# v loaded in k's layout, E turned by VectorE in 32x32 blocks, and the product with v in 18 steps of four 32x32 tiles

## The chip, the cores and the metric

The kernel runs on one core of a Trainium2 chip. The metric is the device time of one execution in microseconds, as the median of several runs. TensorE (PE) multiplies matrices, VectorE (DVE) and ScalarE (ACT) work elementwise, GpSimd (POOL) does a few conversions, and SyncE (SP) issues nearly all transfers, which run on 16 shared DMA engines.

## The reference

Two attentions and two feed-forward blocks, one behind the other. The change lies in the first attention, where 32 "pack" queries p attend to 576 tokens.

```python
# q, k, v: (8, 8, 576, 64) = batch, heads, tokens, head size; p: (8, 8, 32, 64)
def sm_attn(qq, kk, vv):
    s = scale * qq @ kk^T
    a = exp(s - max(s));  a = a / (sum(a) + 1e-9)
    return a @ vv
p_packed = sm_attn(p, k, v)              # 32 x 64 per head
out      = sm_attn(q, p_packed, p_packed)
x = out as (4608, 512)
x = (h * cos(h)) @ w_out          with h = x @ w_in          # 512 -> 2048 -> 512
x = (P(h) / (Q(h) + 1e-6)) @ w_out with h = x @ w_in         # 512 -> 2048 -> 512
```

## The kernel before, in words

The first stage takes the 64 (batch, head) pairs in NG = 16 groups of four heads. In a group the four heads lie side by side on the partitions, 32 each, and each step of a matrix product is made of four small matmuls, one for a head, which are placed on different tiles of TensorE's array.

For a group n the steps are these. `load_k` brings k with 18 consecutive tokens a partition: partition 32h + j holds tokens 18j to 18j + 17 of head h, as one run of 4608 bytes. `load_v` brings v in another layout, with tokens on 96 partitions: three transfers of 32 partitions each, in runs of 6 tokens (1536 bytes). `prep` turns k in 32x32 blocks on VectorE (kT). `s1` computes the scores in two halves of 288 tokens (tile `s` in the profile), takes their maximum (mx), scales it (nb), lets ScalarE form E = exp(...) with its sum (sm), and inverts the sum (rd). `et` turns E on TensorE, in six transposes of 128x96 into PSUM, which ScalarE copies to eT. `pv` multiplies eT with v into one PSUM tile of 128x64; ScalarE scales it by rd into pd and pp. `ppt` turns pd on TensorE (pt), and ScalarE puts it into wl, which the next stage reads.

The loop runs these steps shifted against each other: in its round n come the scores of group n + 1, the loads and the turning of k for later groups, `et(n)`, `pv(n - 1)` and `ppt(n - 2)`. Between them stand the steps of the second attention of batch 0 (qT, ppT, sT, aT, al) and, in every second round, the conversion of a weight tile (st, cvf, w1i). Each engine works off its own row of instructions in order; a scheduler makes these rows when the program is built. SyncE's transfers are issued in order too. Buffers are few: three each for kx and vx, two each for kT, E and eT, and two PSUM tiles for scores.

The stage behind it starts with the matmuls `w<-w1i,wl` (L284), which need all of the first stage's PSUM, so all of its groups. The two feed-forward blocks follow and fill the rest of the time.

Of the kernel before, what the change touches and what calls it, by code (L numbers as in the profile page):

```python
# [9 lines left out]
F32 = mybir.dt.float32  # L10
F32R = mybir.dt.float32r
U32 = mybir.dt.uint32
AF = mybir.ActivationFunctionType
# [7 lines left out]
def pack_attention_moe_moe_kernel(  # L21
# [14 lines left out]
    nc = tc.nc  # L36
# [75 lines left out]
    if True:  # L112
# [18 lines left out]

        def load_v(n):
            b, g = divmod(n, G)
            t = wv.tile([96, 4, 6 * D], F32, tag="vx", bufs=3, name="vx")
            for a in range(3):
                nc.sync.dma_start(
                    out=t[32 * a:32 * a + 32],
                    in_=v[b, 4 * g:4 * g + 4].rearrange("h (j a r) d -> a j h (r d)", a=3, r=6)[a],
                )
            vx_t[n] = t  # L140

        def load_kv(n):
# [31 lines left out]
        kT_t = {}  # L174

        def prep(n):
            b, g = divmod(n, G)
            kT = wk.tile([128, NDB, 6, 3, 32], F32, tag="kT", bufs=2, name="kT")
            kx = kx_t.pop(n)
            for e in range(NDB):  # L180
                nc.vector.transpose(
                    out=kT[:, e].rearrange("p r a j -> p a r j"),
                    in_=kx[:, :, 32 * e:32 * e + 32].rearrange("p (a r) i -> p a r i", a=3),
                )
            kT_t[n] = kT.rearrange("p e r a j -> p e (r a j)")

        def scores(ps, lhs, rhs):
            for hf in range(2):
# [22 lines left out]
        E_t, rd_t = {}, {}  # L211

        def s1(n):
            ps = ps0.tile([128, 2, 512], F32, tag="s1", bufs=2, name="s1")
            scores(ps, pT[:, n], kT_t.pop(n))
            mx = wk.tile([128, 1], F32, tag="mx", bufs=2, name="mx")
            nc.vector.tensor_reduce(out=mx, in_=ps[:, :, 0:HS], op=ALU.max, axis=AX.XY)
            nb = wk.tile([128, 1], F32, tag="nb", bufs=2, name="nb")
            nc.vector.tensor_scalar(out=nb, in0=mx, scalar1=-scale, scalar2=None, op0=ALU.mult)
            E = wk.tile([128, 6, 96], F32, tag="E", bufs=2, name="E")  # L220
            sm = wk.tile([128, 1], F32, tag="sm", bufs=2, name="sm")
            nc.scalar.activation(
                out=E.rearrange("p (t r) x -> p t (r x)", t=2),
                in_=ps[:, :, 0:HS], func=AF.Exp, scale=scale, bias=nb, accum_out=sm,
            )
            rd = wk.tile([128, 1], F32, tag="rd", bufs=3, name="rd")
            nc.vector.tensor_scalar(out=sm, in0=sm, scalar1=1e-9, scalar2=None, op0=ALU.add)
            nc.vector.reciprocal(out=rd, in_=sm)
            E_t[n], rd_t[n] = E, rd

        et_t = {}

        def et(n):
            E = E_t.pop(n)
            ps = ps0.tile([96, 2, 512], F32, tag="et", name="et")
            for r in range(6):
                o = 128 * (r % 3)
                nc.tensor.transpose(ps[:, r // 3, o:o + 128], E[:, r, :], ident)
            eT = wv.tile([96, 6, 128], F32, tag="eT", bufs=2, name="eT")
            nc.scalar.activation(out=eT.rearrange("p (t r) m -> p t (r m)", t=2), in_=ps[:, :, 0:384], func=AF.Copy)  # L240
            et_t[n] = eT

        pd_t = {}
# [1 line left out]
        def pv(n):  # L245
            eT, vx = et_t.pop(n), vx_t.pop(n)
            ps = ps0.tile([128, D], F32, tag="pv", name="pv")

            for r in range(6):
                for h in range(4):  # L250
                    pace[0] = nc.tensor.matmul(
                        out=ps[32 * h:32 * h + 32],
                        lhsT=eT[:, r, 32 * h:32 * h + 32],
                        rhs=vx[:, h, r * D:r * D + D],
                        start=(r == 0),
                        stop=(r == 5),
                        tile_position=(0, 32 * h),
                    )
            rd = rd_t.pop(n)
            pd = wk.tile([128, 2, D], F32, tag="pd", bufs=2, name="pd")  # L260
            nc.scalar.activation(
                out=pd, in_=ps.unsqueeze(1).to_broadcast([128, 2, D]), func=AF.Copy, scale=rd
            )
            pd_t[n] = pd
            nc.scalar.activation(out=pp[:, n], in_=ps, func=AF.Copy, scale=rd)
# [192 lines left out]
        for i in range(at_ld0):  # L458
# [1 line left out]

        tg0 = {"qT": ("kT", 2), "aT": ("E", 2)}
        at = attn2_steps(
            0, wk, lambda nm: ps0.tile([128, 2, 512], F32, tag="s1", bufs=2, name=nm), tg0, lambda: None
        )
        s1(0)
        prep(1)
        for n in range(NG + 2):
            if n >= 3:
                next(at, 1)
            if n + 1 < NG:  # L470
                s1(n + 1)
            if n + 3 < NG:
                load_k(n + 3)
            if n + 2 < NG:
                load_v(n + 2)
                prep(n + 2)
            if n < NG:
                et(n)
            if 1 <= n <= NG:
                pv(n - 1)  # L480
            if n >= 2:
                ppt(n - 2)
            if n % 2 and n <= 2 * EARLY:
                conv_next()
# [429 lines left out]
```

## Time and profile before

| what | us |
|---|---|
| median of 3 runs (lowest, highest) | 1663.2 (1661.97, 1664.64) |
| the profiled execution: time | 1665.62 |
| its span, first to last instruction | 1663.6 |
| TensorE busy | 1595.3 (96%) |
| VectorE busy | 1252.1 (75%) |
| ScalarE busy | 1200.8 (72%) |
| first stage: first scores, first matmul of the next stage | 7.34, 110.26 |

The span is what the trace covers; the time of the same execution is 2.0 us longer. A busy share is an average over stages with different limits, so the first stage has to be read by itself. An instruction's time reaches from its start to its end on its engine; neighbours on one engine overlap a little, so the distance from one start to the next says more on a row of them.

### The profile page before, as it was taken

The page shows a single profiled execution, that of the slowest core. Times are in us where ns is not written, and L with a number is a line of the kernel's source. Part 1 is how long each engine was busy: PE and PEld are TensorE (multiplying, and loading weights), DVE is VectorE, ACT ScalarE, POOL GpSimd, SP SyncE. Part 2 cuts the span into 40 slices and gives each one's busy share as a digit, 9 for nine tenths or more (in the row PEclk, how much of TensorE's full clock was granted, in tenths as well). Part 3 has the DMA queues.
Part 4 walks back from the last instruction along what each step waited for, and adds up shares of the span by engine and source line. Part 5 has one row for each costly group of instructions (what it writes and reads, how often), then busy time and mean ns, then how long its engine had stood idle before and what let it go on. Part 6 is the DMA issues. An engine that isn't in the chain of part 4 may idle for free.

```text
span 1663.6 us, 25747 instructions
## 1 busy us (share of the span) xinstructions
PE 1595.3 (96%) x9792; PEld 1353.8 (81%) x9792; DVE 1252.1 (75%) x1934; ACT 1200.8 (72%) x1973; POOL 158.2 (10%) x120
## 2 busy tenths in 40 slices
PE   6789988999999999999999999999999999999997
PEld 3446668999999999999998888888888888888886
DVE  5745568777868777868558888888888888888886
ACT  3467657676768677768668877877777778787875
POOL 1014330112111112121000000000000000000000
PEclk9889999999999999999999999999999999999999
DMA  9957774344444444445292101010110202020010
GB/s 273 246 151 241 245 213 134 116 142 133 137 133 125 139 144 133 136 127 179 63 303 110 54 24 51 26 51 26 37 40 3 74 1 76 1 76 1 12 40 26
DMA packets 98427, 176.40 MB, mean 106 GB/s; under 512 B 11648, under 2 KB 42880, under 8 KB 98304
## 3 DMA queue, kind: packets, MB, share of 16 engines
q1 hardware_dynamic: 97984, 174.23, 34.4%
q8 instruction: 77, 1.26, 0.3%
q10 hardware_dynamic: 320, 0.52, 0.1%
q14 instruction: 46, 0.38, 0.1%
HBM read 114.36 MB, written 60.36 MB: 105 GB/s over the span
## 4 chain that ended last, share of the span: by engine, by line
PE 75%; DVE 8%; ACT 5%; issue 2%; DMA 2%; POOL 0%; SPq 0%; DVEq 0%; ACTq 0%; POOLq 0%
PE h L773 24%; PE o L860 24%; PE y L634 16%; PE h L580 8%; PE w L307 1%; PE s L192 1%; DVE r L606 1%; ACT r L610 1%; DVE g L612 1%; DVE gl L67 1%; ACT r L611 1%; PE w L284 1%; DVE wq L67 1%; DVE qT L343 1%; DVE sT L383 1%
## 5 line engine op out<-in xcount | busy, mean ns | idle before, releaser
L634 PE MATMUL y<-gh,w1o 128*128 128x288 f32 x2048 | 440.7, 301 | 4.1 <-ACT gh L66 2.6
L773 PE MATMUL h<-x,w 128*128 128x512 f32 x1728 | 422.2, 393 | 0.0
L773 PEld LDWEIGHTS h<-x,w 128*128 128x128 f32 x1728 | 324.2, 188 | 74.3
L634 PEld LDWEIGHTS y<-gh,w1o 128*128 128x128 f32 x2048 | 338.5, 190 | 17.0 <-issue 7.7
L860 PE MATMUL o<-w,g2h 128*128 128x512 f32 x1152 | 332.9, 393 | 1.2 <-ACT g2h L791 1.2
L634 PE MATMUL y<-gl,w1o 128*128 128x288 f32 x1024 | 300.6, 300 | 8.3 <-DVE gl L67 8.2
L860 PEld LDWEIGHTS o<-w,g2h 128*128 128x128 f32 x1152 | 216.2, 188 | 51.1 <-ACT g2h L791 2.1
L580 PE MATMUL h<-ah,wq 128*128 128x288 f32 x1024 | 231.8, 302 | 14.0 <-DVE g L612 13.2
L634 PEld LDWEIGHTS y<-gl,w1o 128*128 128x128 f32 x1024 | 194.6, 190 | 15.5 <-DVE gl L67 11.8
L860 PE MATMUL o<-w,g2l 128*128 128x512 f32 x576 | 199.9, 393 | 0.0
L806 ACT ACTIVATE sq<-h 128x512 f32<-128x512 f32 x144 | 87.6, 608 | 154.6 <-PE h L773 154.6
L580 PEld LDWEIGHTS h<-ah,wq 128*128 128x128 f32 x1024 | 173.1, 190 | 24.2 <-issue 19.2
L808 DVE SCALAR_TENSOR_TENSOR ab<-sq,coef,ab 128x512 f32<-128x512 f32 x144 | 108.2, 751 | 66.0 <-ACT ab L807 65.8
L612 DVE SCALAR_TENSOR_TENSOR g<-h,r 128x576 f32<-128x576 f32 x128 | 95.6, 753 | 79.6 <-ACT r L611 79.0
L580 PE MATMUL h<-al,wq 128*128 128x288 f32 x512 | 151.7, 296 | 0.0
L605 ACT ACTIVATE u<-h,coef 128x576 f32<-128x576 f32 x128 | 94.3, 739 | 74.0 <-PE h L580 73.5
L817 DVE SCALAR_TENSOR_TENSOR ab<-ab,y 128x512 f32<-128x512 f32 x144 | 99.5, 691 | 48.7 <-ACT y L814 48.7
L860 PEld LDWEIGHTS o<-w,g2l 128*128 128x128 f32 x576 | 108.2, 188 | 24.6
L606 DVE SCALAR_TENSOR_TENSOR r<-u,h 128x576 f32<-128x576 f32 x128 | 95.3, 748 | 38.6 <-ACT u L605 38.2
L67 DVE TENSOR_TENSOR gl<-g,gh 128x576 fp32r<-128x576 f32 x128 | 99.7, 780 | 30.4 <-ACT gh L66 28.5
L809 ACT ACTIVATE c<-h,coef 128x512 f32<-128x512 f32 x144 | 114.3, 794 | 8.5 <-DVE g2l L797 8.4
L66 ACT ACTIVATE gh<-g 128x576 fp32r<-128x576 f32 x128 | 87.3, 682 | 40.9 <-DVE g L612 38.2
(98 smaller groups left out, 2315.6 us busy)
## 6 DMA issues: line engine op xcount, KB each, us to landing
x<-yd SPq DMA_DIRECT2D x36, 512.0 KB
w<-w2d SPq DMA_DIRECT2D x68, 256.0 KB
st<-in_moe_w_in_dram SPq DMA_DIRECT2D x32, 512.0 KB
st<-in_moe_w_out_dram SPq DMA_DIRECT2D x32, 512.0 KB
wq<-wd SPq DMA_DIRECT2D x56, 256.0 KB
wd<-wev SPq DMA_DIRECT2D x48, 256.0 KB
kx<-in_k_dram SPq DMA_DIRECT2D x16, 576.0 KB
vx<-in_v_dram SPq DMA_DIRECT2D x48, 192.0 KB
```

Source lines behind the costliest of these rows:

```text
L67: lo_eng.tensor_tensor(out=lo, in0=src, in1=hi.bitcast(F32), op=ALU.subtract)
L580: last_h[0] = nc.tensor.matmul(out=ps[:, u, 0:HS], lhsT=wq[:, g, a, o:o + 128], rhs=a_t[b, g][c][:, hf * HS:hf * HS + HS], start=(i == 0), ...
L605: nc.scalar.activation(out=u, in_=ph, func=AF.Identity, bias=coef[:, 6:7])
L606: nc.vector.scalar_tensor_tensor(out=r, in0=u, scalar=RND, in1=ph, op0=ALU.subtract, op1=ALU.subtract)
L612: nc.vector.scalar_tensor_tensor(out=gt, in0=ph, scalar=2.0 * math.pi, in1=r, op0=ALU.mult, op1=ALU.mult)
L634: nc.tensor.matmul(out=y_t[d][:, 0:HS], lhsT=w1o_s[f // 4][a][:, f % 4, 128 * d:128 * d + 128], rhs=gs[c][:, u], start=(first and u == 0 a ...
L773: nc.tensor.matmul(out=ps, lhsT=w2_s[f][:, 0, a, 128 * kk:128 * kk + 128], rhs=x_t[t, c, kk], start=(i == 0), stop=(i == 3 * NKD - 1),)
L806: nc.scalar.activation(out=sq, in_=ph, func=AF.Square)
L808: nc.vector.scalar_tensor_tensor(out=ab, in0=sq, scalar=coef[:, 5:6], in1=ab, op0=ALU.mult, op1=ALU.add)
L809: nc.scalar.activation(out=c1, in_=ph, func=AF.Identity, scale=coef[:, 3:4], bias=coef[:, 2:3])
L817: nc.vector.scalar_tensor_tensor(out=ab, in0=ab, scalar=QC, in1=y0, op0=ALU.add, op1=ALU.mult)
L860: nc.tensor.matmul(out=o_t[s], lhsT=g2_t[n][a][:, 128 * s:128 * s + 128], rhs=w2_s[f][:, 1, c], start=(f == 0 and i == 0), stop=(f == NFC ...
```

## The change

v is loaded like k: one transfer of 128 partitions with runs of 4608 bytes. E keeps the token order of k, as 18 blocks of 32 columns, and VectorE turns it in 32x32 blocks, from SBUF to SBUF, which leaves the tokens of each head on that head's 32 partitions, as v now has them. The six transposes on TensorE, their PSUM tile and the copy by ScalarE go. The product with v is then a sum over 18 steps with 32 tokens of each head, in place of 6 steps with 96: 72 matmuls with a contraction of 32 rows in place of 24 with 96, each head on its own rows and columns of the array. k is turned by one instruction instead of two, without the reordering of tokens. There is a third PSUM tile for scores, and `et(n)` stands ahead of `prep(n + 2)` in the loop.

```diff
--- before.py
+++ after.py
@@ -131,12 +131,8 @@
 
         def load_v(n):
             b, g = divmod(n, G)
-            t = wv.tile([96, 4, 6 * D], F32, tag="vx", bufs=3, name="vx")
-            for a in range(3):
-                nc.sync.dma_start(
-                    out=t[32 * a:32 * a + 32],
-                    in_=v[b, 4 * g:4 * g + 4].rearrange("h (j a r) d -> a j h (r d)", a=3, r=6)[a],
-                )
+            t = wv.tile([128, C, D], F32, tag="vx", bufs=3, name="vx")
+            nc.sync.dma_start(out=t, in_=v[b, 4 * g:4 * g + 4].rearrange("h (j c) d -> (h j) c d", c=C))
             vx_t[n] = t
 
         def load_kv(n):
@@ -174,15 +170,11 @@
         kT_t = {}
 
         def prep(n):
-            b, g = divmod(n, G)
-            kT = wk.tile([128, NDB, 6, 3, 32], F32, tag="kT", bufs=2, name="kT")
-            kx = kx_t.pop(n)
-            for e in range(NDB):
-                nc.vector.transpose(
-                    out=kT[:, e].rearrange("p r a j -> p a r j"),
-                    in_=kx[:, :, 32 * e:32 * e + 32].rearrange("p (a r) i -> p a r i", a=3),
-                )
-            kT_t[n] = kT.rearrange("p e r a j -> p e (r a j)")
+            kT = wk.tile([128, NDB, C, 32], F32, tag="kT", bufs=2, name="kT")
+            nc.vector.transpose(
+                out=kT.rearrange("p e c j -> p c e j"), in_=kx_t.pop(n).rearrange("p c (e i) -> p c e i", e=NDB)
+            )
+            kT_t[n] = kT.rearrange("p e c j -> p e (c j)")
 
         def scores(ps, lhs, rhs):
             for hf in range(2):
@@ -211,16 +203,16 @@
         E_t, rd_t = {}, {}
 
         def s1(n):
-            ps = ps0.tile([128, 2, 512], F32, tag="s1", bufs=2, name="s1")
+            ps = ps0.tile([128, 2, 512], F32, tag="s1", bufs=3, name="s1")
             scores(ps, pT[:, n], kT_t.pop(n))
             mx = wk.tile([128, 1], F32, tag="mx", bufs=2, name="mx")
             nc.vector.tensor_reduce(out=mx, in_=ps[:, :, 0:HS], op=ALU.max, axis=AX.XY)
             nb = wk.tile([128, 1], F32, tag="nb", bufs=2, name="nb")
             nc.vector.tensor_scalar(out=nb, in0=mx, scalar1=-scale, scalar2=None, op0=ALU.mult)
-            E = wk.tile([128, 6, 96], F32, tag="E", bufs=2, name="E")
+            E = wk.tile([128, C, 32], F32, tag="E", bufs=2, name="E")
             sm = wk.tile([128, 1], F32, tag="sm", bufs=2, name="sm")
             nc.scalar.activation(
-                out=E.rearrange("p (t r) x -> p t (r x)", t=2),
+                out=E.rearrange("p (t c) j -> p t (c j)", t=2),
                 in_=ps[:, :, 0:HS], func=AF.Exp, scale=scale, bias=nb, accum_out=sm,
             )
             rd = wk.tile([128, 1], F32, tag="rd", bufs=3, name="rd")
@@ -231,13 +223,8 @@
         et_t = {}
 
         def et(n):
-            E = E_t.pop(n)
-            ps = ps0.tile([96, 2, 512], F32, tag="et", name="et")
-            for r in range(6):
-                o = 128 * (r % 3)
-                nc.tensor.transpose(ps[:, r // 3, o:o + 128], E[:, r, :], ident)
-            eT = wv.tile([96, 6, 128], F32, tag="eT", bufs=2, name="eT")
-            nc.scalar.activation(out=eT.rearrange("p (t r) m -> p t (r m)", t=2), in_=ps[:, :, 0:384], func=AF.Copy)
+            eT = wv.tile([128, C, M], F32, tag="eT", bufs=2, name="eT")
+            nc.vector.transpose(out=eT, in_=E_t.pop(n))
             et_t[n] = eT
 
         pd_t = {}
@@ -246,15 +233,16 @@
             eT, vx = et_t.pop(n), vx_t.pop(n)
             ps = ps0.tile([128, D], F32, tag="pv", name="pv")
 
-            for r in range(6):
+            for c in range(C):
                 for h in range(4):
+                    r = slice(32 * h, 32 * h + 32)
                     pace[0] = nc.tensor.matmul(
-                        out=ps[32 * h:32 * h + 32],
-                        lhsT=eT[:, r, 32 * h:32 * h + 32],
-                        rhs=vx[:, h, r * D:r * D + D],
-                        start=(r == 0),
-                        stop=(r == 5),
-                        tile_position=(0, 32 * h),
+                        out=ps[r],
+                        lhsT=eT[r, c],
+                        rhs=vx[r, c],
+                        start=(c == 0),
+                        stop=(c == C - 1),
+                        tile_position=(32 * h, 32 * h),
                     )
             rd = rd_t.pop(n)
             pd = wk.tile([128, 2, D], F32, tag="pd", bufs=2, name="pd")
@@ -460,7 +448,7 @@
 
         tg0 = {"qT": ("kT", 2), "aT": ("E", 2)}
         at = attn2_steps(
-            0, wk, lambda nm: ps0.tile([128, 2, 512], F32, tag="s1", bufs=2, name=nm), tg0, lambda: None
+            0, wk, lambda nm: ps0.tile([128, 2, 512], F32, tag="s1", bufs=3, name=nm), tg0, lambda: None
         )
         s1(0)
         prep(1)
@@ -471,11 +459,11 @@
                 s1(n + 1)
             if n + 3 < NG:
                 load_k(n + 3)
+            if n < NG:
+                et(n)
             if n + 2 < NG:
                 load_v(n + 2)
                 prep(n + 2)
-            if n < NG:
-                et(n)
             if 1 <= n <= NG:
                 pv(n - 1)
             if n >= 2:
```

TensorE's row around groups 4 to 6 of the first stage. `s_` tiles are scores (from kT in the first attention, from qT in the second), et the transposes of E, pv the product, pt the turning of pd. Before:

```order
L202 MATMUL s_375<-kT,pT 32x288 x16
L238 MATMUL et<-ident,E 96x128 x6
L251 MATMUL pv<-vx,eT 32x64 x24
L271 MATMUL pt<-ident,pd 128x128
L202 MATMUL s_467<-kT,pT 32x288 x16
L238 MATMUL et<-ident,E 96x128 x6
L251 MATMUL pv<-vx,eT 32x64 x24
L271 MATMUL pt<-ident,pd 128x128
L202 MATMUL s_544<-qT,ppT 32x288 x16
L202 MATMUL s_565<-kT,pT 32x288 x16
```

The same place now:

```order
L194 MATMUL s_435<-kT,pT 32x288 x16
L239 MATMUL pv<-vx,eT 32x64 x72
L259 MATMUL pt<-ident,pd 128x128
L194 MATMUL s_565<-kT,pT 32x288 x16
L239 MATMUL pv<-vx,eT 32x64 x72
L259 MATMUL pt<-ident,pd 128x128
L194 MATMUL s_680<-qT,ppT 32x288 x16
L194 MATMUL s_701<-kT,pT 32x288 x16
```

The six transposes between the scores and the product are gone, and the product has three times as many matmuls; nothing else moved.

VectorE's row around groups 4 and 5. mx and nb are the maximum and its scaling, sm and rd the sum of E (which waits for ScalarE's exp) and its inverse, cvf the weight conversion, qT a step of the second attention. Before:

```order
L217 TENSOR_REDUCE mx<-s_375 128x1
L343 STREAM_TRANSPOSE qT<-qx 128x18x2x32
L219 TENSOR_SCALAR nb<-mx 128x1
L79 TENSOR_SCALAR cvf<-st_136 128x512
L84 SCALAR_TENSOR_TENSOR cvf<-st_136,cvf 128x512
L227 TENSOR_SCALAR sm<-sm 128x1
L228 RECIPROCAL rd<-sm 128x1
L217 TENSOR_REDUCE mx<-s_467 128x1
L181 STREAM_TRANSPOSE kT<-kx 128x3x6x32 x2
L219 TENSOR_SCALAR nb<-mx 128x1
L227 TENSOR_SCALAR sm<-sm 128x1
L228 RECIPROCAL rd<-sm 128x1
```

The same place now:

```order
L209 TENSOR_REDUCE mx<-s_435 128x1
L331 STREAM_TRANSPOSE qT<-qx 128x18x2x32
L211 TENSOR_SCALAR nb<-mx 128x1
L219 TENSOR_SCALAR sm<-sm 128x1
L220 RECIPROCAL rd<-sm 128x1
L79 TENSOR_SCALAR cvf<-st_131 128x512
L84 SCALAR_TENSOR_TENSOR cvf<-st_131,cvf 128x512
L227 STREAM_TRANSPOSE eT<-E 128x576
L209 TENSOR_REDUCE mx<-s_565 128x1
L174 STREAM_TRANSPOSE kT<-kx 128x18x2x32
L211 TENSOR_SCALAR nb<-mx 128x1
L219 TENSOR_SCALAR sm<-sm 128x1
```

A turn of E stands at the end of each group's round, and the weight conversion, which stood between nb and sm, now stands behind rd. The kT that is turned between mx and nb belongs to the next group in the rounds of groups 5 and 7, and to the one behind the next from group 8 on, in both kernels. Behind the first stage the rows of all engines are the same in both.

## Rows read from the trace of the kernel before

**Rows 1.** Stretches in us: busy time (instructions) of each engine, granted clock, DMA share, GB/s.

```profile
15.00:20.00 5.00, 4.97 (x54) 2.25 (x50) 2.78 (x8) 2.60 (x4) 0.00 (x0) 0.70 1.02 406
...
41.80:45.30 3.50, 3.50 (x35) 1.50 (x31) 0.00 (x0) 0.65 (x4) 0.00 (x0) 0.51 1.06 267
...
20.00:95.00 75.00, 59.05 (x1089) 32.60 (x1079) 50.26 (x104) 33.99 (x88) 7.71 (x6) 0.89 0.98 246
...
85.00:90.00 5.00, 5.00 (x38) 2.17 (x38) 0.96 (x2) 0.52 (x3) 0.00 (x0) 0.54 1.00 202
...
110.00:1663.60 1553.60, 1513.98 (x8336) 1309.46 (x8336) 1187.77 (x1793) 1154.04 (x1850) 145.39 (x105) 0.99 0.31 96
```

**Rows 2.** Timeline of SyncE's transfers: first issue us, us to the last, count.

```profile
10.89 0.33 SPq L129 DMA_DIRECT2D kx<-in_k_dram  x1
...
81.10 15.05 SPq L136 DMA_DIRECT2D vx<-in_v_dram  x12
```

**Rows 3.** Waits of SyncE, 8 to 96 us: us in total, times, longest.

```profile
SPq L136 <- DMA vx<-in_v_dram: 11.0, 18, 1.2
```

**Rows 4.** Timeline of TensorE: start us, us, tile, count [idle before <-releaser].

```profile
7.34 3.99 PE L202 MATMUL s<-kT,pT 32*32 32x288 f32 x32 [7.34 <-DVE pT L169]
...
95.03 2.14 PE L202 MATMUL s<-kT,pT 32*32 32x288 f32 x32
97.10 0.86 PE L238 MATMUL et<-ident,E 128*96 128x128 f32 x6
97.89 0.88 PE L251 MATMUL pv<-vx,eT 96*32 96x64 f32 x48
98.70 0.33 PE L271 MATMUL pt<-ident,pd 128*128 128x128 f32 x1
98.96 2.14 PE L202 MATMUL s<-kT,pT 32*32 32x288 f32 x32
...
110.26 2.79 PE L284 MATMUL w<-w1i,wl 128*64 128x512 f32 x5 [0.58 <-ACT wl L275]
```

**Rows 5.** Timeline of VectorE, columns as in rows 4.

```profile
13.10 1.44 DVE L181 STREAM_TRANSPOSE kT<-kx 128x576 f32<-128x576 f32 x2 [4.25 <-DMA kx<-in_k_dram]
14.46 0.72 DVE L217 TENSOR_REDUCE mx<-s 128x1 f32<-128x576 f32 x1
...
20.90 1.44 DVE L181 STREAM_TRANSPOSE kT<-kx 128x576 f32<-128x576 f32 x2 [1.48 <-DMA kx<-in_k_dram]
...
93.98 1.43 DVE L181 STREAM_TRANSPOSE kT<-kx 128x576 f32<-128x576 f32 x2
95.33 0.11 DVE L219 TENSOR_SCALAR nb<-mx 128x1 f32<-128x1 f32 x1
96.40 0.15 DVE L227 TENSOR_SCALAR sm<-sm 128x1 f32<-128x1 f32 x1 [0.96 <-ACT E L222]
96.59 0.16 DVE L228 RECIPROCAL rd<-sm 128x1 f32<-128x1 f32 x1
...
101.17 0.76 DVE L217 TENSOR_REDUCE mx<-s 128x1 f32<-128x576 f32 x1 [0.79 <-PE s L202]
```

**Rows 6.** Waits of VectorE from its first to its last maximum, 14.4 to 101.3 us.

```profile
DVE kT L181 <- DMA kx<-in_k_dram: 7.4, 4, 3.8
DVE sT L366 <- PE s L202: 7.0, 2, 5.0
DVE mx L217 <- PE s L202: 6.9, 5, 4.5
DVE sm L227 <- ACT E L222: 6.0, 7, 1.0
DVE qT L343 <- DMA qx<-in_q_dram: 1.9, 1, 1.9
```

**Rows 7.** Groups by line, 0 to 110 us: busy us, mean ns | idle before.

```profile
L251 PEld LDWEIGHTS pv<-vx,eT 96*32 96x32 f32 x768 | 12.9, 117 | 12.4 <-issue 7.4 <-ACT E L222 3.0 <-ACT pp L265 1.5
```

## The prediction

> **What bounds the kernel now.** I read the stretches first. From 110 us to the end TensorE is busy 1514.0 of 1553.6 us [rows 1]: that is the two feed-forward stages, where the diff touches nothing, and the order of all five engines behind the first stage is the same row for row in both kernels. So whatever the change does it does before 110.26 us, when the first matmul of the next stage starts [rows 4], and it moves the end by as much as it moves that start.
>
> Inside the first stage the next view is the DMA's share. From 20 to 95 us it is 0.98 at 246 GB/s [rows 1]: the transfers bound most of the stage, at a poor rate. The rate depends on what moves. The k load issued at 10.89 us is not there until 20.90 [rows 2, 5]; ahead of it in the queue stand another k load and two weight loads, so 15 to 20 us is k and weights, and it runs at 406 GB/s. From 81.10 on SyncE issues twelve v pieces and nothing else [rows 2]; 85 to 90 us runs at 202 GB/s with the same full share [rows 1]. v, in pieces of 32 partitions and 1.5 KB runs, goes at half the rate of k in 128 partitions and 4.5 KB runs. SyncE itself waits on earlier landings, 18 times on v alone [rows 3], and VectorE and TensorE stand behind it. VectorE's waits from its first maximum to its last are 7.4 us for k, 1.9 us for q, and 7.0 + 6.9 us for scores that TensorE gave late [rows 6]. Only the last groups, from some 93 us, run at TensorE's pace: scores 2.07 us (95.03 to 97.10), transposes of E 0.79, the product with v 0.81, pt 0.26, together 3.93 us a group [rows 4].
>
> **The change, part by part.**
> *Loads.* v is 16 x 576 KB = 9.44 MB: 46.7 us at 202 GB/s, 23.2 us at k's 406. The transfers lose about 23 us of work, and with it most of their hold: the 18.5 MB moved from 20 to 95 us would take 45 us at 406. The bounds are 202 (no change) and 406; I take 406, since v then has k's own layout. The k load of group 1 lands sooner too: VectorE turns it at 13.10 us after a wait of 4.25 [rows 5], with v(0) and parts of v(1) ahead of it or beside it; px has landed by 7 us (the first scores, behind its transposition, start at 7.34 [rows 4]), and from there two loads of 576 KB at 406 GB/s are 2.9 us. So kT(1) starts at about 10.0 and the first maximum at 11.4 in place of 14.46; the first scores end at 11.33 [rows 4], just in time.
>
> *TensorE.* 0.79 us of transposes go. The product has 72 matmuls in place of 24. The rows count each f32 matmul twice: 48 records start within 0.81 us (97.89 to 98.70), 67 ns for each of a tile's 12 [rows 4]. A tile now has 36: 2.43 us. The low bound is the streaming alone: scores pass 8 records of 288 columns per tile in 2.07 us, so 64 columns are 57 ns and 36 records 2.07 us. I take 2.43, the nearer row. TensorE's round is then 2.07 + 2.43 + 0.26 = 4.76 us, 0.83 more than now.
>
> *ScalarE.* Sixteen evacuations go; ScalarE is not what anyone is behind for long, so I count nothing.
>
> *VectorE.* It gets sixteen turns of E. Two turns of 128x576 take 1.35 us from start to next start (93.98 to 95.33 [rows 5]), so 0.68 each. kT is one instruction instead of two over the same elements: nothing. The order shows two more things: the weight conversion now stands behind rd instead of between nb and sm, so VectorE waits for ScalarE's exp in ten of the first fifteen groups (groups 2 to 7 and 11 to 14) instead of seven. One such wait is 0.96 us [rows 5]; ten are 9.6 us against 6.0 now [rows 6].
>
> *The sum.* VectorE's time from first to last maximum is 101.17 - 14.46 = 86.7 us. Off go 7.4 + 1.9 + 7.0 + 6.9 = 23.2 us of waits for transfers and late scores; on come 15 x 0.68 = 10.2 us of turns and 3.6 us of exp waits: 77.3 us. The last maximum starts at 11.4 + 77.3 = 88.7 us. Behind it stands the tail, now 9.2 us (last scores done at 101.1, next stage at 110.26 [rows 4]). With its waits kept it becomes 9.2 - 2 x 0.79 + 3 x (2.43 - 0.81) = 12.5 us; bare work, three products and what follows the last one now, is about 10. I take 11. That gives 99.7 us if nothing else stalls.
>
> Two things will. VectorE's round without extra work is 0.76 + 1.35 + 1.07 + 0.19 + 0.16 + 0.68 = 4.2 us [rows 5], below TensorE's 4.76: in some six plain groups VectorE waits up to 0.55 us, 3.3 us at most and nothing where kT runs two groups ahead; I take 2. And after a gap TensorE's granted clock falls: 0.51 in 41.8 to 45.3 us [rows 1], the lower of its two levels, 1.2 of 2.4 GHz, right behind a wait for v. A spell of 3.5 us costs up to 1.7 us; I put one on the path. The stage then ends at about 103.4 us, **7 us sooner**.
>
> The profiled execution took 1665.62 us for a span of 1663.6; the median of the runs is 1663.2, 2.4 below it. Taking 7 us off the median gives 1656.2 us. About 0.2%, 3.3 us, can be told from no change.
>
> **A rule against it.** Now four tiles of the product share rows and differ in columns; then they differ in both, and all four add into one PSUM bank. The scores already do just that, four 32x32 tiles into the bank of a half, and 32 records pass in 2.07 us; one after another they would need four times that, 8.3 us [rows 4]. So I price the tiles as side by side. The Trainium skill's "TensorEngine Tiling (Array Packing)", Restrictions and Gotchas, says that different row tiles cannot access the same PSUM bank at the same time; by it the product would be serial, which is the last rival below. This case's scores disagree with it, at 2.07 us against 8.3.
>
> **Rivals.**
> *VectorE and TensorE hold each other up.* Both now have some 80 us of work before the last maximum (TensorE: 11.4 + 17 x 2.07 + 12 x 0.26 + 13 x 2.43 = 81.3 us on the clock, against 88.7). Five stalls or low-clock spells of 1.7 us instead of one bring the stage to its present end: 1660 to 1666. For it: the exp wait stands bare in VectorE's in-order row, and around groups 4 to 7 kT is turned only one group ahead. Against: TensorE's gaps of today are waits for transfers.
>
> *The work packs better.* With no low-clock spell, the product at 2.07 us, a tail of 10, the stage ends at 97 to 99.5, the first matmuls of the next stage no longer run at the low clock: 11 to 14 us off, 1649 to 1652.
>
> *v stays slow.* If v's 202 GB/s is not from its layout, the transfers end where they end now, and the tail grows by 1 to 3 us: 1663 to 1666. Against it: k's rate in the same queue.
>
> *The product is dearer than the room.* TensorE's whole row is 11.4 + 35.2 + 3.1 + 0.5 + 2.1 us and sixteen products: 52.3 + 16 x p. At p = 3.6 us the stage ends where it ends now; above that the kernel is slower. A load of weights for the product lasts 117 ns [rows 7]; if a tile's 36 loads are not hidden behind its own matmuls, p = 36 x (0.117 + 0.067) = 6.6 us, the stage ends at 158, and the time is about 1711. Fully serial tiles would be 144 x 67 ns = 9.7 us, end 207.5: 1760. For it: a load then serves a third of the rows, so there are three times as many. Against: the 48 records of today pass at 17 ns each, load and matmul together, and the scores' 32x32 tiles run four abreast.
>
> **How the numbers follow.** My forecast, 3.4 to 11 us off: 0.56. Better packing: 0.14. Mutual holding: 0.16. v slow: 0.05. The product too dear: 0.09, of which serial tiles 0.03. Faster by over 0.2%: 0.56 + 0.14 = 0.70. Slower: 0.09 and part of v slow, 0.11. Within: 0.19. The range reaches from the better packing's end, 1648, to 1664, where mutual holding and slow v are mostly in; beyond it lie the dear product and some of those two, under 0.2.
>
> **What would show it.** Right: k and v loads alike, windows of 5 us near 400 GB/s in the first 20 us and a DMA share well below 0.9 after 30; VectorE's waits for k and q gone and those for exp near ten; VectorE busy 80% or more from 11 to 90 us; the product's 144 records in 2.1 to 2.5 us; the next stage's first matmul at 100 to 107 us. Wrong: a product over 3 us, or v windows still near 200 GB/s, or TensorE's clock at half in more than three spells before 100 us.

## The result and the profile after

The changed kernel takes 1674.87 us (median; 1674.34 to 1680.97), the kernel before 1662.59 (1659.55 to 1664.64): a ratio of 1.0078, 95% interval 1.0050 to 1.0106. It is **slower by 12 us** where 7 us faster was predicted. The profiled execution took 1674.34 us for a span of 1672.5.

The stretches of the changed kernel, with the columns of [rows 1]:

```profile
15.00:20.00 5.00, 5.00 (x72) 2.41 (x68) 3.52 (x8) 2.93 (x5) 0.00 (x0) 0.71 1.03 417
14.50:18.00 3.50, 3.50 (x36) 1.55 (x32) 2.60 (x5) 2.11 (x3) 0.00 (x0) 0.52 1.04 421
20.00:95.00 75.00, 59.49 (x2025) 41.14 (x2017) 53.57 (x100) 23.33 (x74) 6.41 (x5) 0.93 0.68 234
24.70:28.10 3.40, 3.40 (x45) 1.95 (x37) 2.76 (x5) 0.57 (x2) 1.28 (x1) 0.50 0.53 144
41.80:45.20 3.40, 3.40 (x114) 3.07 (x109) 2.08 (x3) 0.14 (x1) 0.00 (x0) 0.50 0.50 197
86.10:89.50 3.40, 3.08 (x37) 1.57 (x41) 1.09 (x3) 1.40 (x6) 0.00 (x0) 0.51 0.34 102
113.40:116.90 3.50, 3.25 (x114) 2.78 (x102) 0.00 (x0) 0.55 (x3) 0.00 (x0) 0.51 0.02 5
122.00:1672.50 1550.50, 1511.07 (x8337) 1306.42 (x8336) 1187.84 (x1793) 1151.58 (x1851) 144.99 (x105) 0.99 0.31 97
```

The transfers did what was predicted: 417 GB/s with v among them, and a DMA share of 0.68 from 20 to 95 us where it was 0.98 [rows 1]. Behind the first stage the order is that of before, and TensorE is busy 1511.1 of 1550.5 us there. But the product breaks off, again and again. TensorE's timeline, columns as in [rows 4]; it shows the start, the last quarter and the end of the stage:

```profile
19.84 1.96 PE L239 MATMUL pv<-vx,eT 32*32 32x64 f32 x127
24.41 0.52 PE L239 MATMUL pv<-vx,eT 32*32 32x64 f32 x17 [2.62 <-issue]
...
100.32 1.72 PE L239 MATMUL pv<-vx,eT 32*32 32x64 f32 x91
103.88 0.86 PE L239 MATMUL pv<-vx,eT 32*32 32x64 f32 x44 [1.84 <-issue]
...
106.89 2.19 PE L239 MATMUL pv<-vx,eT 32*32 32x64 f32 x144
109.01 0.33 PE L259 MATMUL pt<-ident,pd 128*128 128x128 f32 x1
109.83 0.64 PE L239 MATMUL pv<-vx,eT 32*32 32x64 f32 x31 [0.49 <-ACT pp L253]
113.19 3.05 PE L239 MATMUL pv<-vx,eT 32*32 32x64 f32 x113 [2.72 <-issue]
...
122.60 2.67 PE L272 MATMUL w<-w1i,wl 128*64 128x512 f32 x8 [0.58 <-ACT wl L263]
```

Where nothing breaks it and the clock is full, the product passes in 2.12 us (106.89 to 109.01). Elsewhere it breaks off in its middle, with its operands there since its first record, and TensorE stands for 0.6 to 2.7 us on "issue", a wait for nothing that another engine does. The next stage starts at 122.60 in place of 110.26 [rows 4]: 12.3 us later, as much as the medians differ. The two profiled spans differ by less, 8.9 us: what stands behind that start took 1549.9 us in this execution and 1553.3 in that of before, a difference within the spread of either kernel's runs. The waits of the stage, for TensorE (0 to 123 us) and VectorE (11 to 115 us), columns as in [rows 6]:

```profile
PE pv L239 <- issue: 14.8, 8, 2.7
...
PE pv L239 <- ACT pp L253: 5.3, 5, 2.1
...
PE s L194 <- issue: 2.6, 2, 2.0
```

```profile
DVE sm L219 <- ACT E L214: 11.5, 14, 1.0
DVE mx L209 <- PE s L194: 11.2, 6, 4.7
DVE kT L174 <- DMA kx<-in_k_dram: 3.4, 4, 1.9
DVE sT L354 <- PE s L194: 2.6, 2, 1.5
```

VectorE's waits for q went and those for k fell from 7.4 us [rows 6] to 3.4; those for exp grew, as predicted, though in 14 places where ten were counted. Its waits for scores did not go (13.8 us, 13.9 before [rows 6]): TensorE is late again, from a new cause. On issue it waits 17.4 us in ten places. In the trace of before there is one such wait up to 111 us:

```profile
PE pv L251 <- issue: 1.7, 1, 1.7
```

**Where the breaks lie.** Stretches of the changed kernel from 0 to just before a break; the counts in brackets behind the first two busy times are TensorE's matmul and load records:

```profile
0.00:24.40 24.40, 11.47 (x223) 5.75 (x223) 11.84 (x27) 4.32 (x8) 2.55 (x7) 0.93 0.90 320
0.00:35.40 35.40, 20.32 (x476) 11.76 (x477) 20.04 (x40) 6.79 (x17) 3.83 (x8) 0.90 0.87 307
0.00:40.60 40.60, 23.53 (x604) 13.96 (x604) 22.14 (x45) 8.78 (x23) 5.11 (x9) 0.92 0.88 311
...
0.00:103.80 103.80, 75.64 (x2383) 50.16 (x2384) 68.17 (x131) 29.36 (x87) 10.26 (x13) 0.93 0.70 241
0.00:113.10 113.10, 81.74 (x2636) 54.67 (x2637) 74.06 (x141) 32.63 (x98) 12.89 (x15) 0.94 0.69 236
```

From break to break there are 253, 128, ..., 253 matmul records, with as many loads: all ten breaks lie whole multiples of 127 matmuls apart, within 1, that is of some 254 records, whether a product or a score is cut. That is a property of the instruction stream, not of data. The queues of the page say what comes in such pieces (packets, MB, share), of before and then of after:

```profile
q8 instruction: 77, 1.26, 0.3%
```

```profile
q8 instruction: 88, 1.44, 0.4%
```

Eleven packets more, 0.18 MB or some 16 KB each, for 1440 matmuls and as many loads more (9792 and 11232 of each on the two pages): a packet for 262 records. Hence **theory A**: TensorE's instructions come in blocks of some 256, and the change makes it use them up faster than they come. **Theory B**, the prediction's own rival: the engines hold each other up (exp waits that stand bare, one pv buffer, low clock), and the number of records costs only its passing.

### The profile page after: what moved, and what is told of

Same layout as the page of the kernel before. It is cut to its first block, busy times and chain, and to the rows that moved or that the text cites. A ratio compares the mean times of both kernels' runs of the same rounds, so it can differ in the third digit from the quotient of the medians.

```text
span 1672.5 us, 28544 instructions
## 1 busy us (share of the span) xinstructions
PE 1599.3 (96%) x11232; PEld 1366.5 (82%) x11232; DVE 1261.9 (75%) x1934; ACT 1186.0 (71%) x1957; POOL 157.9 (9%) x120
## 4 chain that ended last, share of the span: by engine, by line
PE 77%; DVE 10%; ACT 6%; issue 3%; DMA 2%; POOL 1%; SPq 1%; DVEq 0%; ACTq 0%; POOLq 0%
PE h L761 24%; PE o L848 23%; PE y L622 15%; PE h L568 8%; PE pv L239 2%; PE s L194 2%; PE w L295 1%; PE s L184 1%; ACT r L598 1%; DMA yd<-yh 1%; DVE r L594 1%; DVE gl L67 1%; ACT r L599 1%; DVE g L600 1%; PE w L272 1%
## 5 line engine op out<-in xcount | busy, mean ns | idle before, releaser
L568 PE MATMUL h<-ah,wq 128*128 128x288 f32 x1024 | 230.6, 301 | 14.1 <-DVE g L600 13.4
```

The costliest lines, as they stand in the source:

```text
L568: last_h[0] = nc.tensor.matmul(out=ps[:, u, 0:HS], lhsT=wq[:, g, a, o:o + 128], rhs=a_t[b, g][c][:, hf * HS:hf * HS + HS], start=(i == 0), ...
```

## Experiments

The runs at a glance; the next stage starts at 110.26 us before and at 122.60 in the change. Records a group are matmuls and loads together, counted up to that start and divided by the 16 groups: 182 before and 362 in the change, of these 2 x 144 for the product and 2 x 32 for the scores, the rest for pt and the second attention. The expectations put these counts 3 to 4 higher.

| run | records a group | waits on issue, us (places) | next stage starts | ratio to before (95%) |
|---|---|---|---|---|
| e1_tiny: before + 48 tiny matmuls | 374 | 21.0 (13) | 141.3 | 1.0211 (1.0185 to 1.0237) |
| e2_bf16: product in bf16 | 218 | 1.6 (1) | 95.0 | 0.9924 (0.9897 to 0.9951) |
| e2b_bf16_twice | 362 | 23.1 (14) | 120.2 | 1.0094 (1.0073 to 1.0115) |
| e3_v_one_dma: before's load alone | 182 | 6.2 (5) | 110.4 | 0.9993 (0.9976 to 1.0010) |
| e5_pv2: two pv buffers | 362 | 22.8 (13) | 127.4 | 1.0090 (1.0064 to 1.0116) |
| e7_wide_scores | 314 | 13.7 (10) | 116.5 | 1.0036 (1.0015 to 1.0057) |
| e10_v_short_runs | 362 | 17.3 (11) | 120.9 | one run |
| e11_v_32_partitions | 362 | 29.7 (15) | 139.4 | one run |
| e15_pairs: half the matmuls | 218 | none | 118.1 | 1.0023 (1.0008 to 1.0038) |
| e17_pairs_pv2 | 218 | none | 114.1 | 1.0026 (1.0012 to 1.0041) |
| e18_exp_ahead: order alone | 362 | 22.3 (12) | 126.7 | 1.0092 (1.0061 to 1.0123) |
| e19_pairs_exp_ahead | 218 | none | 101.8 | 0.9942 (0.9922 to 0.9963) |

**Records into the kernel before.**

```
             ps = ps0.tile([128, 128], F32, tag="pt", name="pt")
+            for i in range(48):
+                r = slice(32 * (i % 4), 32 * (i % 4) + 32)
+                nc.tensor.matmul(
+                    out=ps[r, 0:1], lhsT=ident[r, 0:32], rhs=ident[r, 0:1],
+                    start=True, stop=True, tile_position=(32 * (i % 4), 32 * (i % 4)),
+                )
```

> The kernel before, with 48 matmuls of a single column (32x32 tiles, four positions) put into each pt tile ahead of its transposition, which overwrites them: TensorE's records per group go from some 186 to some 378, as many as the change brings (365); transfers, E's turn and the product stay those of before. Theory A (TensorE's instructions arrive too slowly for three times as many small matmuls): waits on issue of 1 to 3 us appear on TensorE, at least six of them and 8 us or more in all, and the next stage's first matmul starts at 117 to 126 us in place of 110.26, so 7 to 16 us slower. Theory B (the change loses its time to waits between the engines: bare waits for exp, one pv buffer, VectorE and TensorE in turn; the number of records costs no more than 17 ns each): 192 more records are at most 3.3 us a group on an engine that waits for transfers until 93 us; no more than two waits on issue, and 0 to 6 us slower.

Its waits of TensorE, 0 to 142 us, and the start of the next stage:

```profile
PE pt L273 <- issue: 9.9, 4, 5.9
PE pv L251 <- issue: 5.6, 4, 2.4
PE s L202 <- issue: 5.5, 5, 2.0
...
141.30 3.14 PE L290 MATMUL w<-w1i,wl 128*64 128x512 f32 x8 [0.58 <-ACT wl L281]
```

The old kernel, with its slow loads and its own product, now has the breaks, in scores, product and tiny matmuls alike: A. The stage ends 31 us later, twice the most that A gave: beside 21.0 us of breaks the tiny matmuls are busy 19.1 us in all, and TensorE's clock stands at 0.66 from 80 to 95 us.

**Records out of the changed kernel.** The upper halves of the words are read as bf16, so the product is coarser; the last two lines are the second kernel's alone, which makes it twice over.

```
-                        lhsT=eT[r, c],
-                        rhs=vx[r, c],
+                        lhsT=eT[r, c].bitcast(BF16).rearrange("p (m t) -> p m t", t=2)[:, :, 1],
+                        rhs=vx[r, c].bitcast(BF16).rearrange("p (d t) -> p d t", t=2)[:, :, 1],
...
-            for c in range(C):
+            for c in list(range(C)) * 2:
```

> The changed kernel with the product taken from the upper halves of E's and v's words, read as bf16, so with a coarser product: each of its 72 matmuls is one load and one matmul instead of two and two, so 144 records fewer per group (some 221 instead of 365) and the columns stream in half the time. Loads, E's turn, order and buffers are those of the change. Theory A: the waits on issue on TensorE (17.4 us in ten places) go down to 4 us or less, and the next stage starts at 97 to 105 us in place of 122.6, so 18 to 25 us faster than the changed kernel and 5 to 13 faster than before. Theory B: only the product's time goes, 1 us a group, partly hidden: waits on issue stay near 17 us, the next stage starts at 110 to 120 us.

> As the bf16 product, but made twice, the second over the first: as many records as the changed kernel has (288 for the product), each streaming half as long, about 1.2 + 1.2 us. Theory A: the supply of instructions sets the pace whatever the columns cost: waits on issue of 14 us or more again, the next stage starts at 117 to 127 us. Theory B: TensorE has the same busy time as in the changed kernel or less and the same waits between engines: 115 to 123 us, and if e2_bf16 has lost its waits on issue, this one has none either.

TensorE's waits, and behind them one unbroken product from its timeline, of the single product and of the double one:

```profile
PE pv L240 <- ACT pp L254: 16.9, 11, 5.0
...
PE pv L240 <- issue: 1.6, 1, 1.6
...
41.35 0.79 PE L240 MATMUL pv<-vx,eT 32*32 32x64 bf16 x72
```

```profile
PE pv L240 <- issue: 16.9, 9, 3.1
...
PE s L195 <- issue: 6.2, 5, 3.0
PE pv L240 <- ACT pp L254: 4.8, 6, 1.8
...
49.13 1.39 PE L240 MATMUL pv<-vx,eT 32*32 32x64 bf16 x144
```

With 144 records fewer the breaks are gone, all but one, and the stage ends 27.6 us sooner, at 95.0 and so sooner than A's 97 to 105. Not all of that is breaks: the product passes in 0.79 us where 2.12 were needed, up to some 21 us over 16 groups. The double product settles it. It passes in 1.39 us, still less than the change's 2.12, and the breaks are all back, and so is the end. That end, 120.2, lies in A's range and in B's; the breaks decide for A. Loads, order and buffers are the same, the streaming is shorter than in the change, and the breaks follow the count.

**The load alone, in the kernel before.**

```
-            for a in range(3):
-                nc.sync.dma_start(
...
+            nc.sync.dma_start(out=t, in_=v[b, 4 * g:4 * g + 4].rearrange("h (x r) d -> x h (r d)", r=6))
-            kT = wk.tile([128, NDB, 6, 3, 32], F32, tag="kT", bufs=2, name="kT")
+            kT = wk.tile([128, NDB, 6, 32, 3], F32, tag="kT", bufs=2, name="kT")
```

> The kernel before with only its v load changed: one DMA over 96 partitions instead of three over 32 (token 6x+r on partition x; kT's columns are put in the order r, j, a instead of r, a, j, so that E matches). Product, transpositions and records stay those of before. Both theories: v's transfers go at 300 to 400 GB/s and the DMA share falls below 0.85 after 40 us. Theory A: with 186 records per group TensorE's instructions come in time, no more than three waits on issue, and the freed transfers bring the next stage to 97 to 105 us: 5 to 13 us faster than before. Theory B: with the transfers gone the same waits between engines come up as in the change: 107 to 114 us, within 4 us of before.

```profile
20.00:95.00 75.00, 59.28 (x1050) 32.48 (x1046) 52.27 (x103) 32.42 (x85) 7.74 (x6) 0.89 1.00 242
85.00:90.00 5.00, 5.00 (x48) 1.96 (x41) 0.74 (x5) 1.61 (x6) 0.00 (x0) 0.50 0.95 192
```

Both theories were wrong on the load: over 96 partitions v goes at 192 GB/s where it is alone, no faster than over 32. The transfers stayed the bound and the time the same, so the end says nothing between A and B. One thing goes against A: it allowed three waits on issue and there are five, 6.2 us, again near multiples of 127 matmuls apart (378, 127, 125 and 126), at the count of before, which has one. So the count is not all that makes a break; what else does stays open.

**What made v slow.** Two other ways to load it in the changed kernel: short runs on 128 partitions, long runs on 32.

```
+            for x in range(3):
+                nc.sync.dma_start(
+                    out=t[:, 6 * x:6 * x + 6],
+                    in_=v[b, 4 * g:4 * g + 4].rearrange("h (j c) d -> (h j) c d", c=C)[:, 6 * x:6 * x + 6],
+                )
...
+            for h in range(4):
+                nc.sync.dma_start(
+                    out=t[32 * h:32 * h + 32], in_=v[b, 4 * g + h].rearrange("(j c) d -> j c d", c=C)
+                )
```

> The changed kernel with each v load in three DMAs of six tokens a partition: still 128 partitions, but runs of 1.5 KB instead of 4.5. If the run's length made before's v slow, stretches of v go at 200 to 250 GB/s again; if the 32 partitions did, they stay at 350 to 410 GB/s. The stage's end stays within 4 us of 122.6 by theory A, which puts it down to TensorE's instructions; by theory B it is 3 to 8 us later where v is slow.

> The changed kernel with each v load in four DMAs of 32 partitions with the long runs of 4.5 KB. If the 32 partitions made before's v slow, stretches of v go at 200 to 250 GB/s; if the run's length did, at 350 to 410 GB/s. The stage's end stays within 4 us of 122.6 by theory A; by theory B it is 3 to 8 us later where v is slow.

Stretches at full share, the first two of the short runs, then of the 32 partitions:

```profile
15.00:20.00 5.00, 5.00 (x101) 2.49 (x96) 3.46 (x7) 2.78 (x5) 0.00 (x0) 0.78 1.01 403
20.00:25.00 5.00, 2.24 (x120) 1.94 (x113) 2.88 (x8) 1.46 (x4) 0.00 (x0) 0.90 1.04 405
```

```profile
10.00:15.00 5.00, 1.45 (x14) 0.19 (x4) 0.71 (x1) 0.00 (x0) 0.00 (x0) 1.00 1.03 232
20.00:25.00 5.00, 3.85 (x159) 2.75 (x159) 2.64 (x5) 0.83 (x2) 0.00 (x0) 1.00 1.05 245
```

The partitions make the rate, not the run's length. The Trainium skill ("SBUF — State Buffer", Door 1: The DMA port swizzle) says that a transfer's rate goes by how many of 16 ports its partitions reach, and that 32 of them reach half; 232 to 245 against 403 to 417 GB/s agrees. It does not explain the 192 of 96 partitions, which stays open. The other half of the expectation missed for both theories: with slow loads the changed kernel ends its stage 17 us later, not within 4 (A) or 3 to 8 (B). VectorE waits 12.2 us for k (3.4 in the change), and the breaks are longer too, 29.7 us in all and up to 5.0 (2.7 in the change). This is one run; that full DMA queues delay the blocks would fit it, but was not tested by itself. Full queues are not needed for a break: the last one of the change, 1.2 us before 120.36, falls where the DMA share is 0.02 (118 to 121 us).

**One buffer more; wider scores.** The first takes B's wait for pv away (s1 goes back to two buffers); the second takes 48 records a group out of the scores instead of the product, by a pT with zeros off its diagonal blocks.

```
-            ps = ps0.tile([128, D], F32, tag="pv", name="pv")
+            ps = ps0.tile([128, D], F32, tag="pv", bufs=2, name="pv")
...
-        pT = wv.tile([128, NG, NDB, M], F32, name="pT")
+        pT = wv.tile([128, NG, NDB, 4, M], F32, name="pT")
```

> The changed kernel with two PSUM buffers for pv, and two instead of three for the scores (PSUM is full): the product no longer waits until ScalarE has read the one before (5.3 us in five places in the changed kernel). Theory A (TensorE's instructions arrive too slowly): the waits on issue take over, 15 us or more of them stay and the next stage starts at 118 to 126 us. Theory B (waits between the engines): they go and nothing takes their place: 113 to 118 us.

> The changed kernel with fewer and wider score matmuls: p is turned into a block-diagonal pT of 128 columns once at the start, so that a group's scores are 4 matmuls over 128 rows and 128 columns instead of 16 in four 32x32 tiles, which stream as many columns per record (16 records instead of 64, some 317 per group instead of 365). It costs VectorE six more turns at the start, some 3 us, and shifts the engines' order a little. Theory A: 768 records fewer are three blocks of 256, each 3.5 to 5 us in the changed kernel: the next stage starts at 108 to 117 us. Theory B: TensorE's busy time is the same, and the start is later: 122 to 127 us.

The buffer removed the 5.3 us and the breaks took their place, 22.8 us of them: the stage ends at 127.4, later than A's 126. The wide scores brought the end to 116.5, within A's 108 to 117; their breaks are in the product alone.

**Half the matmuls at full precision.** Two heads stand side by side in E with zeros across, so that 64x64 tiles do (mb is 0 in a head's own half, -8000 in the other, whose exp is then 0); the second kernel has two pv buffers as well.

```
+            nc.vector.tensor_scalar(out=nb, in0=mb, scalar1=mx, scalar2=scale, op0=ALU.subtract, op1=ALU.mult)
+            for x in range(2):
+                nc.scalar.activation(
+                    out=E[:, x].rearrange("p (t c) j -> p t (c j)", t=2),
+                    in_=ps[:, :, 0:HS], func=AF.Exp, scale=scale, bias=nb[:, x:x + 1],
...
-                for h in range(4):
-                    r = slice(32 * h, 32 * h + 32)
+                for h in range(2):
+                    r = slice(64 * h, 64 * h + 64)
```

> The changed kernel with half the product's matmuls at full precision: the exp is written twice, once with -1000 added to the exponent of the odd heads and once of the even ones, so that E, turned, holds two heads beside each other with zeros across; the product is then 18 steps of two 64x64 tiles, 36 matmuls (144 records in place of 288, some 221 per group in all). It costs ScalarE a second exp of some 1.1 us a group and VectorE a turn twice as long, 0.7 us more a group, so VectorE has 11 us more to do and the way from a maximum to its product is 1.8 us longer. Theory A (TensorE's instructions arrive too slowly): no more than three waits on issue, and in spite of the added work the next stage starts at 105 to 114 us, 8 to 17 us before the changed kernel's 122.6. Theory B (waits between the engines): the added work comes on top, 124 to 136 us.

> The pairs kernel (36 full-precision matmuls of 64x64 tiles, no waits on issue) with two PSUM buffers for pv and two for the scores. Its TensorE waited 19.5 us in twelve places until ScalarE had read the pv tile before, behind the two exps of the next group. Theory A: with the instructions in time these waits are what is left, and go: the next stage starts at 103 to 112 us in place of 118.1, and the kernel is 0.1 to 0.6% faster than before. Theory B, that the engines' waits take each other's place: 114 to 119 us, still slower than before.

The first kernel's waits of TensorE, 0 to 119 us:

```profile
PE pv L249 <- ACT pp L263: 19.5, 12, 3.7
PE s L194 <- DVE coef L147: 7.3, 1, 7.3
PE s L194 <- DVE kT L174: 2.5, 2, 1.7
```

The breaks are gone altogether, at full precision and with 2.3 us for the product, as in the change: A. But the stage ends at 118.1 and 114.1, past A's ranges, the second just inside B's. So B has a part: with instructions there, TensorE waits for pv to be read, and with that mended VectorE's waits for exp, 19.5 us in 14 places, are left. These are larger than the change's 11.5 us: the pairs kernel does each exp twice.

**VectorE's row alone, and both.** A group's sum and turn are held until the next group's nb has gone out, so that exp runs beside other work (until and nbi are that nb's instruction): in the changed kernel, then in the pairs kernel with two pv buffers.

```
-            nc.vector.tensor_scalar(out=sm, in0=sm, scalar1=1e-9, scalar2=None, op0=ALU.add)
+                hold(nc.vector.tensor_scalar(out=sm, in0=sm, scalar1=1e-9, scalar2=None, op0=ALU.add), until)
-            nc.vector.transpose(out=eT, in_=E_t.pop(n))
+            hold(nc.vector.transpose(out=eT, in_=E_t.pop(n)), nbi[0])
```

> The changed kernel with VectorE's row alone put differently: a group's sum and E's turn are held until the next group's maximum and nb have gone out, so that ScalarE's exp runs beside VectorE's other work. Records, loads and product stay those of the change. The waits for exp, 11.5 us in the changed kernel, go to 3 us or less. Theory A (TensorE's instructions arrive too slowly): the waits on issue stay at 14 us or more and the next stage starts at 116 to 123 us. Theory B (the bare exp waits are the loss): it starts at 108 to 114 us.

> The pairs kernel with two pv buffers and the same hold: VectorE's 19.5 us of waits for exp go to 4 us or less, and there are no waits on issue. Both theories agree that this must be sooner than 114.1 us; theory A, with nothing late any more but VectorE's own work (87.8 us busy of the first 125), says 99 to 107 us, and the kernel is 0.2 to 0.7% faster than before at full precision. If what is taken from the exp waits comes back as other waits of VectorE, 110 to 114 us.

VectorE's waits, 10 to 118 us, in the changed kernel with the hold:

```profile
DVE mx L211 <- PE s L194: 24.2, 9, 5.2
DVE sT L364 <- PE s L194: 6.6, 2, 3.5
...
DVE sm L225 <- ACT E L216: 0.2, 1, 0.2
```

and in the pairs kernel with the hold, 10 to 102 us; behind it that kernel's stretch from 20 to 80 us:

```profile
DVE kT L174 <- DMA kx<-in_k_dram: 3.8, 3, 2.1
DVE mx L215 <- PE s L194: 3.8, 5, 1.2
...
DVE sm L233 <- ACT E L223: 0.3, 1, 0.3
```

```profile
20.00:80.00 60.00, 52.18 (x1147) 35.84 (x1144) 56.41 (x92) 28.33 (x86) 7.22 (x5) 0.97 0.79 282
```

In the change the 11.5 us of exp waits go to 0.2 and come back as waits for scores, 13.8 to 30.8 us: nothing gained, the stage even later, at 126.7 and so past both ranges. The breaks, 22.3 us of them, set the pace. Where they do not, the same hold takes the stage from 114.1 to 101.8. That kernel takes 1653.71 us (its runs of before 1664.46, ratio 0.9942): at full precision it beats the kernel before, and so the change too. VectorE's work bounds it now (56.4 of 60 us).

**The limit that is left.** The bf16 product with two pv buffers, with wide scores, and with the buffers and the hold.

> The bf16 product with two PSUM buffers for pv and two for the scores. With the instructions in time, the longest sum of waits of the bf16 kernel's TensorE is for ScalarE to read pv, 16.9 us in eleven places. Theory A: those waits are next in line and go; the next stage starts at 89 to 94 us in place of 95.0. If VectorE's row is next instead (busy 18.9 and 17.9 of 20 us from 40 to 80 us in the bf16 kernel), the stage ends within 1.5 us of 95.0.

> The bf16 product with the wide score matmuls: 48 records a group fewer again, some 173. Theory A: instructions no longer bind at 221, so fewer bring nothing: the next stage starts at 94 to 100 us, VectorE's six more turns at the start included. If they still bind at 221, it starts at 86 to 92 us.

> The bf16 product with two pv buffers and the same hold. The bf16 kernels' VectorE waits 7.7 us for exp and is busy 18.9 and 18.0 of 20 us from 40 to 80 us. If these waits are on the path, the next stage starts at 85 to 90 us in place of 93.1; if VectorE's work alone sets it, within 2 us of 93.

They start the next stage at 93.1, 90.0 and 92.5 us, with ratios of 0.9880, 0.9885 and 0.9887 (each known to some 0.002 or 0.003). The buffers took 1.9 us, the slow end of the first reading: the 16.9 us of waits for pv went, and 12.7 us of waits until ScalarE has emptied pt came instead. The wide scores reached 90.0, sooner than A's 94 to 100 and in the range given for instructions that still bind; but the waits for pv are gone in it too, and the bf16 kernel had only 1.6 us on issue to lose, so the gain is not shown to be one of instructions. The hold, which should have brought 85 to 90 if exp waits were on the path, brings nothing here: VectorE is busy 18.6 of 20 us from 40 to 60 us, and 6.1 us of breaks in five places are back.

Taken together, A's forecast of the breaks came true in seven of the eight runs that had one (not in e3), and its forecast of the stage's end in five of fourteen. That the number of records brings the breaks is shown; what they cost in the end is not reckoned by it.

## Why the prediction was wrong, point by point

*Loads: right.* 417 GB/s, share 0.68, and the rate is from the layout. One piece missed: kT(1) began at 12.8 and not 10.0 us, its load landing late, so the first maximum came at 14.1 instead of 11.4.

*The product's size: right.* 2.43 us was priced, 2.12 measured, near the low bound. Serial tiles would take the 9.7 us of the last rival. The bank rule of the Trainium skill ("TensorEngine Tiling (Array Packing)", Restrictions and Gotchas), by which they would be serial, is not borne out.

*ScalarE: counted at nothing.* TensorE waits 5.3 us until pv has been read; taken away, it brought nothing (e5), but 4.0 us in the pairs kernel and 1.9 in the bf16 one, where the breaks are gone.

*The turns and the exp waits: right in size.* VectorE waits 11.5 us for exp, in 14 places, against 9.6 reckoned from ten.

*"Two things will [stall]": this is the step that failed.* The sum let the product's records cost their passing and nothing else. The prediction's argument against a dear product, 48 records at 17 ns each, was read from 48 records that no break fell into. Three times as many of them a product, 362 instead of 182 records a group, also have to be brought, and the list of stalls had no term for that. It is 17.4 us of breaks. Low-clock stretches, of which the sum put one on the path, follow some of them: four of the five shown above begin within 1.1 us of a break's end (24.41, 40.70, 86.42, 113.19). One sign that the prediction set for being wrong came, the clock at half in more than three spells before 100 us: there are four. A sign of being right did not: VectorE is busy 56.0 of 79 us from 11 to 90, 71% and not 80. But the clock is not what sets the change behind: its mean up to the next stage's start is 0.93, and 0.89 in before. First maximum 2.7 us late and 17.4 us of breaks, less what they hide of each other and of the 2 + 1.7 us reckoned, stand against the 19.2 us between 103.4 and 122.60; the shares are not separated.

*The rivals.* "Mutual holding" named the exp wait rightly, but for the wrong kernel: alone it is worth nothing here (e18). It is worth 12.3 us in the pairs kernel (e17 to e19), whose exp is done twice, and 0.6 us in the bf16 one (e12 to e20). Its place, 1660 to 1666, was too kind. "Dearer than the room" had the right quantity, the number of records, and the wrong mechanism, weight loads that are not hidden.

*The end without the breaks.* With fewer records and the exp waits covered, the stage ends at 101.8 us and the kernel takes 1653.7: 103.4 and 1656.2 were predicted. That the two lie so close is in part luck: that kernel has a second exp, turns twice as long, another order and two pv buffers, none of them in the sum. The kernel nearest to the change, e2_bf16, ends the stage at 95.0 with a product that is 1.3 us shorter. What is shown is that the room which was forecast exists, and that the change as written cannot reach it.

The trace had two signs: one break of 1.7 us in before, and 77 instruction packets. The first alone did not show the size.

## What to carry to other kernels

When a change cuts one big matmul into several small ones, count the records per microsecond, not only their passing: here 218 a group came in time or nearly so, and 314 did not. The pace between breaks fits that. In the change 127 matmuls and their loads are used up in 3.2 to 3.5 us (35.45 to 38.65, 98.57 to 102.04), and the next break follows. As many take some 5.7 us in the last groups of before and some 5.5 in e19's, and no break falls there (estimates, from 87 matmuls in 3.93 us [rows 4] and 105 in 4.57). A wait on "issue" in the middle of one tile's matmuls, at a constant distance in records, is the sign. Two limits that lie close together must be taken away together: at full precision, mending either alone (e17, e18) left the kernel slower than before, and both made it 0.6% faster (e19). In bf16 fewer records alone made it 0.8% faster, and the hold added nothing.

## What the runs showed of the hardware

TensorE's instructions arrive in packets of some 16 KB, one for some 256 records, and short matmuls outrun them: neighbouring breaks one packet apart lie 5.25 us (35.45 to 40.70) and 5.31 us (98.57 to 103.88) apart in the change, and down to 3.4 us (112.73 to 116.13) in e2b. How far ahead a packet is fetched, and what sets that spacing, stays open.

The Trainium skill ("Runtime: NRT & Kernel Launch", Instruction fetch mechanics) says that instructions are refilled in 16 KiB blocks of 256 while the engine runs, and that the cost of crossing a boundary is mostly hidden. The trace agrees on the size of the blocks and not on the cost: 17.4 us in ten of them in the change, 21.0 us in thirteen in e1.
